# Tile 1's first layer ahead of tile 0's second in a fused attention and MLP kernel, both as seven products of quarters

## The chip, the cores and the metric

The kernel runs on one core of a Trainium2 chip. The metric is the device time of one launch in microseconds (us): 263.96 us, median of three runs (263.92 to 264.14). A core has five engines that work at the same time, each through its own list of instructions in order: TensorE (PE, with PEld for its weight loads), VectorE (DVE), ScalarE (ACT), GpSimd (POOL) and SyncE (SP). They wait for each other through semaphores. Transfers between the chip's memory (DRAM) and the core's SBUF are issued by POOL, SP or ACT and done by 16 DMA engines. Products are summed up in PSUM, which has eight banks of 512 float32 for each of 128 partitions.

## The reference

```python
kv = np.einsum('bhsd,bhse->bhde', k, v)            # 8 batches, 8 heads, 576 rows, 64 wide
out = np.einsum('bhsd,bhde->bhse', q, kv)
rms = np.sqrt(np.mean(out * out, axis=-1, keepdims=True) + 1e-06)
x = (out / rms * g_norm)                           # transposed to 4608 rows of 512
h = x @ w_in                                       # 512 -> 2048
g = h * (1.0 / (1.0 + np.exp(-1.702 * h)))
return (g @ w_out)                                 # 2048 -> 512
```

## The kernel before

**Tiles.** The 4608 rows are worked in nine tiles of 512: tile t has the first 512 rows of batch t, and tile 8 collects the last 64 rows of all eight batches (`x_rem`, the "rest"). Each tile has a first layer (x times w_in, then the gate on ACT, into `gT`) and a second layer (gT times w_out, collected in `osb` and stored). The attention of batch t+1 runs among the products of tile t.

**Plain layers.** Tile 0 has both layers plain, tile 1 the first: 64 products 512 wide each. `Hidden.mm` (L419) issues one of the first layer, `project` (L756) one of the second. w_in's columns are counted in blocks of 128, 0 to 15.

**Layers as seven products of quarters.** All other layers take each matrix as 2 x 2 quarters and form the product from seven products of quarters instead of eight, with sums of quarters made on DVE before and behind (`SevenIn`, L482, for the first layer, in four groups of columns; `Seven`, L558, for the second). Each product of quarters is 4 (first layer) or 16 (second) matmuls 256 wide, 112 in a layer. In a plan, "35" is group 3, product 5. DVE makes the sums of weights once: `ws` of w_in (`w_in_sum`, L439, products 3, 5, 6 and 7), `tw` of w_out (`weight_sum`, L552); sums of x for each tile (`xS`, L462), and sums of gT (`gS`, L580). In a group, ACT or DVE copies a bank out of PSUM (L480), DVE adds banks (L544, L546), ACT gates (L510). In the second layer ACT keeps three results in the tile `qf` (L617); DVE's sums (L625) and one copy (L628) place the four quarters in `osb`. The products 1, 6, 7 and 4 add up in one bank, "x", so each waits until the one before it is kept or placed.

**Order.** The order is written out by hand. `dense` (L725) runs both layers of a tile; the dictionaries u1 and u2 say behind which product a piece of other work is issued (`at1`, `at2`, L940 and L943). All engines take their instructions in the order in which they are issued here, and the tile framework adds the waits: for data, and for a buffer of a pool to come free.

**Attention of batches 0 and 1.** They are loaded by pairs of heads, c = 0 to 3, to `kraw`, `vbuf` and `qraw`. For batch 1 DVE packs q (L96), PE transposes it (L403) and DVE copies it to `qT` (L409); PE makes kv (L221), DVE copies it to `kvb` (L357); PE makes the output (L254), ACT its square (L272), PE adds up by a product with ones ("ss", L329), ACT takes the root (L331), and DVE applies it, which gives x (`apply`, L339 and L343). In tile 0's second layer this stands at steps 9 to 60 of 64.

**Later batches** come through DMA transposes (`transpose_q`, L242): `rows` (L275), `add_up`, `roots`, `turn` (L309), and a DMA transpose of x.

**g_norm** (`g_col`) is applied to x for batch 0 alone. For the rest it is multiplied into w_in, once, behind tile 0's first layer (`scale_w_in`, L188).

**Loads.** POOL issues them: batch 0, w_in in parts, then from L879 w_out and batch 1 in turn, and `load_q` and `load_kv` for batch 2 and on.

**Buffers.** One `gT`, two `osb`, two `qf`, one `gS`; PSUM in pools ps_a (3 banks), ps_h (3) and ps_o (2).

Of the kernel before, what the change touches and what calls it, by code (L numbers as in the profile page):

```python
# [16 lines left out]
def kernel(  # L17
# [27 lines left out]
    GROUP = 6  # L45
# [19 lines left out]
    qbuf = const.tile([P, NPAIR * NJ * P], F16)  # L65
    kraw = const.tile([P, NPAIR, 2 * NJ * D], F16)
# [61 lines left out]
    for n in "kqv":  # L128
        if n != "q":
            rows = stage.tile([P, 6, 2 * P], F32, name="qf", tag="qf", bufs=2)  # L130
# [39 lines left out]
    load_w_in(10, 13)  # L170
    load_w_in(13, FO)
# [16 lines left out]
    def scale_w_in(ko, engine):  # L188
        w = w_in_sb[:, ko]
        if engine is nc.scalar:  # L190
            engine.activation(w, w, AFT.Copy, scale=g_col)
        else:
            engine.tensor_scalar_mul(w, w, g_col)

    class Attention:
# [14 lines left out]
        def kv(self, c):  # L210
            if c % self.KEEP == 0:
                self.kvp = ps_a.tile([P, NPAIR, D], F32, name="kvp", tag="att")
# [123 lines left out]
        def apply(self, c):  # L336
            o, rs, n = self.o[c]
            if c < NPAIR and self.b == 0:
# [12 lines left out]
    class Early(Attention):  # L351
        KEEP = 2
# [12 lines left out]
    class First(Early):  # L365


        ss_pool = (ps_o, "o")
# [23 lines left out]
    class Second(Early):  # L392


        ss_pool = rest_pool = (ps_h, "hT")

# [42 lines left out]
    def w_in_sum(n):  # L439

        a11, a12, a21, a22 = quarters(w_in_sb, slice(0, HF * P), slice(0, KH))
        op, a, b = (
            (nc.vector.tensor_add, a21, a22),
            (nc.vector.tensor_sub, ws[:, 0], a11),
            (nc.vector.tensor_sub, a11, a21),
            (nc.vector.tensor_sub, a12, ws[:, 1]),
        )[n]
        op(ws[:, n], a, b)

    class Sums:  # L450


        def __init__(self, t, x):
            x = x if t < B else x.rearrange("p c (j r) -> p c j r", j=J)
# [103 lines left out]
    class Seven:  # L558
# [3 lines left out]
        LAST = (1, 5, 6, 2, 3, 7, 4)  # L562

        def __init__(self, t, gT):
            self.t, self.gT = t, gT
            self.s = spool.tile([P, 4, HF, 2 * P], F16, name="gS", tag="gS")
            self.bank, self.kept = {}, None

        def sums(self, i0, i1, which=(0, 1, 2, 3)):
# [41 lines left out]
        def keep(self, name, mo, as_):  # L611
            ps, m = self.ready(name, mo)
            if self.kept is None:
                k = stage.tile([P, 6, HN], F32, name="qf", tag="qf", bufs=2)
# [4 lines left out]
        def place(self, name, mo, with_, i, j):  # L619
# [9 lines left out]
            if self.t == B:  # L629
# [3 lines left out]
                elif i == 1:  # L633
                    store_rest(2 + mo, j * HN, (j + 1) * HN)
            elif self.t in HALVED and j == 1 - i:
                store(self.t, 2 * i, 2 * i + 2)

        def run(self, units2):
            n = 0
            self.banks("z", 0)  # L640
            for p in self.LAST if self.t == B else self.ORDER:
# [41 lines left out]
    def hid_seven(t, hid, seven, units1):  # L683
# [8 lines left out]

        gates = []
        for n, step in enumerate(todo.steps):
# [12 lines left out]
            for i0, i1, which in todo.ready.get(n, ()):  # L707
                seven.sums(i0, i1, (which,))
# [7 lines left out]

        left = {n: [lambda x=x: late(x) for x in steps] for n, steps in todo.late.items()}
        end = lambda: seven.sums(HF - 2, HF, (0,))
# [6 lines left out]
    def dense(t, units1, units2, group, deep, hid=None):  # L725
        hid = hid or Hidden(t)
        gT = hid.gT
        seven = None if deep else Seven(t, gT)
        cols = range(FO) if deep else [f for i in range(HF) for f in (i, HF + i)]
        ready = {} if deep else {8: (0, 4), 13: (4, 6), 15: (6, 8, (0,))}  # L730
        if group and t:
            order = [(ko, fo) for part in ((0, 3, 1, 2), range(4, group)) for ko in (0, 1) for fo in part]
            order += [(ko, fo) for ko in range(2, KO) for fo in range(group)]
            for ko, i in order:
                pool = (ps_h, "hT") if i < 3 else (ps_a, "att") if i == 3 else (ps_o, "o")
                hid.mm(ko, cols[i], *pool)
            for i in range(group):
                hid.gate(cols[i])
        left = {}
        if t >= SEVEN:  # L740
            left = hid_seven(t, hid, seven, units1)
            cols = ()
        for i, fo in enumerate(cols):
            if i >= group:
                for ko in range(KO):
                    hid.mm(ko, fo)
                hid.gate(fo)
            for u in units1.get(i, ()):
                u()
            if i in ready:  # L750
                seven.sums(*ready[i])

        osb = osbs[t] = opool.tile([P, 4, DM], F32, name="osb", tag="osb")
        os = {}

        def project(mo, fo):  # L756
            if fo == 0:
                pool, tag = (ps_h, "hT") if mo < 2 else (ps_o, "o")
                os[mo] = pool.tile([P, DM], F32, name="o", tag=tag)
            nc.tensor.matmul(  # L760
                os[mo],
                gT[:, fo, mo * P : (mo + 1) * P],
                w_out_sb[:, fo, :],
                start=(fo == 0),
                stop=(fo == FO - 1),
            )
            if fo == FO - 1:
                copy = nc.scalar.copy if mo % 2 else nc.vector.tensor_copy
                copy(osb[:, mo, :], os[mo])

        if deep:
            steps = [(mo, 4 * i + k) for i in range(3) for mo in range(4) for k in range(4)]
            steps += [(mo, f + k) for f in (12, 14) for mo in range(2) for k in range(2)]
            steps += [(mo, 12 + k) for mo in (2, 3) for k in range(4)]
            for n, (mo, fo) in enumerate(steps):
                project(mo, fo)
                for u in units2.get(n, ()):
                    u()
        else:
            later = plan(t).later if t >= SEVEN else {6: ((6, 8, 1),), 30: ((6, 8, 2), (6, 8, 3))}  # L780
            later = {
                n: [lambda x=x: seven.sums(x[0], x[1], (x[2],)) for x in xs] for n, xs in later.items()
            }
            for n, us in units2.items():
                later.setdefault(n, []).extend(us)
            for n, us in left.items():
                later[n] = us + later.get(n, [])
            seven.run(later)
        if t < EARLY:

            n = 0
            while n < SM:
                mo, j, p = n // P, n // PE_, n % PE_
                m = min((mo + 1) * P, (j + 1) * PE_) - n
                nc.sync.dma_start(
                    out=out[t * S : (t + 1) * S, :][bass.DynSlice(NJ * p + j, m, step=NJ), :],
                    in_=osb[n % P : n % P + m, mo, :],
                )
                n += m
        elif t < B and t not in HALVED:  # L800
            store(t, 0, J)
# [87 lines left out]
    load_w_out(14, FO)  # L889

    osbs = {}
    SEVEN = 2
# [26 lines left out]
    FIRST = {  # L919
        "rows": (1, 7, 14, 20),  # L920
        "add_up": (5, 12, 18, 26),
        "table": 21,
        "roots": (32, 32),
        "turn": (33, 34, 35, 36),
    }

    def plan(t):
        return LATER if t < B - 1 else LAST_TWO
# [7 lines left out]
    for t in range(NT):  # L936
        b = t + 1
        u1, u2 = {}, {}

        def at1(i, f, *args):  # L940
            u1.setdefault(i, []).append(lambda: f(*args))

        def at2(i, f, *args):  # L943
            u2.setdefault(i, []).append(lambda: f(*args))  # L944

        def of(b, name, *args):
            return lambda: getattr(live[b], name)(*args)

        if t == 0:
            at1(7, of(0, "out", NPAIR))  # L950
            at2(4, setattr, a0, "ss_pool", Attention.ss_pool)
            at2(4, of(0, "ss", NPAIR, True))
            at2(4, of(0, "apply", NPAIR))
            at1(8, start, 1)
            at2(5, scale_w_in, 0, nc.scalar)
            at2(6, scale_w_in, 1, nc.scalar)
            at2(33, weight_sum, 0)
            at2(33, scale_w_in, 2, nc.vector)
            at2(34, scale_w_in, 3, nc.vector)
            for n, at in ((2, 35), (0, 39), (1, 40)):  # L960
                at2(at, w_in_sum, n)
            for l in range(2):
                at1(9, nc.vector.memset, kvd[l], 0.0)
            at1(13, load_q, 2)
            for c in range(NPAIR):
# [75 lines left out]
```

## Time and profile before

| | us |
|---|---|
| median of three runs | 263.96 |
| the profiled execution's own time | 263.92 |
| its span, first to last instruction of the program | 262.1 |

| stretch of the span | what PE works on |
|---|---|
| 0 to 16.3 | batch 0's attention, first products |
| 16.3 to 29.0 | tile 0's first layer |
| 29.0 to 47.3 | tile 0's second layer, batch 1's attention among it |
| 47.3 to 62.1 | tile 1's first layer, batch 2's kv |
| 62.1 to 75.5 | tile 1's second layer |
| 75.5 to 208.2 | tiles 2 to 6, 26.6 each |
| 208.2 to 257.4 | tiles 7 and 8 |

Times in the views are microseconds from the span's start, unless marked ns. "L530" is a line of the kernel before. A row of the lines view has line, engine, operation, tiles, shapes and count, then the busy time, the mean ns of one, and the idle time of the engine ahead of them with what ended it. "To landing" is the time from the issue of a DMA until its semaphore tells that the data is there.

### The profile page before, as it was taken

To read this page: it belongs to the slowest core of one execution; us is meant where nothing else is said; L and a number is where in the kernel's file an instruction comes from. 1 tells how busy PE (TensorE), PEld (TensorE's weight loads), DVE (VectorE), ACT (ScalarE), POOL (GpSimd) and SP (SyncE) were. 2 spreads that over 40 slices of the span, in tenths; PEclk is the share of its full clock that TensorE was granted. 3 is DMA by queue.
4 is the path that set the end of the run, shared out by engine and by line. 5 is a ranking of instruction groups with operands and counts; after the bars stand their busy time and mean duration, and the time that the engine had idled before them with its cause. 6 is when DMAs were issued, how large, how long until landed. Compare 5 with 4: busy or idle time off the path is not lost.

```text
span 262.1 us, 6210 instructions
## 1 busy us (share of the span) xinstructions
PE 253.6 (97%) x2556; PEld 204.3 (78%) x2556; DVE 185.1 (71%) x324; ACT 173.6 (66%) x308; POOL 43.7 (17%) x68
## 2 busy tenths in 40 slices
PE   6899999999999999999999999999999999999992
PEld 5434554447888988898889988998899888888882
DVE  1540378868768995899589958995899587567831
ACT  3459836776649963996489748974798469737810
POOL 8863242005005001400050005000000000000000
PEclk9999999999999999999999999999999999999998
DMA  7999999999989946996899769946600620021005
GB/s 173 197 199 205 205 203 177 217 206 130 163 180 172 221 58 160 117 240 83 145 154 196 102 157 150 237 54 154 165 0 8 156 83 0 3 100 63 0 3 160
DMA packets 59806, 35.32 MB, mean 135 GB/s; under 512 B 31554, under 2 KB 57154, under 8 KB 59650
## 3 DMA queue, kind: packets, MB, share of 16 engines
q0 software_dynamic: 28608, 18.17, 50.1%
q1 hardware_dynamic: 30768, 16.36, 27.1%
q8 instruction: 20, 0.33, 0.5%
q10 hardware_dynamic: 402, 0.39, 0.5%
q14 instruction: 8, 0.07, 0.1%
HBM read 36.70 MB, written 9.44 MB: 176 GB/s over the span
## 4 chain that ended last, share of the span: by engine, by line
PE 92%; DMA 4%; POOL 1%; DVE 0%; issue 0%; ACT 0%; ACTq 0%
PE o L648 37%; PE h L530 33%; PE hT L422 10%; PE o L760 5%; PE kvp L221 2%; DMA vbuf<-in_v_dram 2%; DMA qraw<-in_q_dram 2%; PE outR L281 2%; PE ss L329 1%; PE outT L254 0%; PE q L403 0%; PE outT L258 0%; POOL kraw L89 0%; ACT sq L272 0%; DVE osb L628 0%
## 5 line engine op out<-in xcount | busy, mean ns | idle before, releaser
L648 PEld LDWEIGHTS <-gS 128*128 128x128 f16 x512 | 49.8, 98 | 5.5
L510 ACT ACTIVATE gT<-h 128x512 f16<-128x512 f32 x84 | 46.2, 605 | 5.1 <-PE h L530 5.1
L530 PEld LDWEIGHTS <-ws 128*128 128x128 f16 x448 | 43.8, 98 | 5.1
L648 PE MATMUL o<-tw,gS 128*128 128x256 f16 x384 | 46.3, 273 | 0.0
L530 PE MATMUL h<-xS,ws 128*128 128x256 f16 x336 | 45.3, 273 | 0.0
L648 PEld LDWEIGHTS <-gT 128*128 128x128 f16 x384 | 37.1, 98 | 4.2
L530 PEld LDWEIGHTS <-w_in_sb 128*128 128x128 f16 x336 | 32.5, 98 | 3.9
L648 PE MATMUL o<-w_out_sb,gT 128*128 128x256 f16 x256 | 33.3, 273 | 0.0
L422 PE MATMUL hT<-xT,w_in_sb 128*128 128x512 f16 x128 | 28.9, 379 | 0.0
L625 DVE TENSOR_TENSOR osb<-o,qf 128x512 f32<-128x512 f32 (+1 forms) x25 | 16.7, 668 | 15.6 <-PE o L648 12.8
L530 PE MATMUL h<-xT,w_in_sb 128*128 128x256 f16 x192 | 27.1, 273 | 0.0
L89 POOL DMA_DIRECT2D kraw<-in_k_dram x11 | 8.1, 733 | 106.3 <-PE kvp L221 87.8
L580 DVE TENSOR_TENSOR gS<-gT 128x512 f16<-128x512 f16 (+2 forms) x34 | 22.0, 653 | 4.5 <-ACT gT L431 3.9
L544 DVE TENSOR_TENSOR h<-h,s 128x512 f32<-128x512 f32 x28 | 19.5, 698 | 7.4 <-PE h L530 5.6
L422 PEld LDWEIGHTS <-w_in_sb 128*128 128x128 f16 x128 | 12.3, 98 | 15.4 <-issue 0.9
L431 ACT ACTIVATE gT<-hT 128x512 f16<-128x512 f32 x32 | 17.6, 613 | 7.0 <-PE hT L422 7.0
L546 DVE TENSOR_TENSOR s<-h,s 128x512 f32<-128x512 f32 x28 | 19.4, 692 | 4.0 <-PE h L530 3.3
L331 ACT ACTIVATE rs<-ss,eps_t 128x512 f32<-128x512 f32 (+1 forms) x16 | 9.2, 584 | 16.4 <-PE ss L329 16.3
L510 ACT ACTIVATE gT<-s 128x512 f16<-128x512 f32 x28 | 17.3, 628 | 1.2 <-DVE s L546 1.2
L944 ACT ACT_TABLE_LOAD x14 | 18.0, 1283 | 0.3
L681 POOL DMA_DIRECT2D out_dram<-osb x2 | 1.1, 562 | 94.1 <-DVE osb L625 94.1
L760 PE MATMUL o<-w_out_sb,gT 128*128 128x512 f16 x64 | 16.7, 380 | 0.0
(93 smaller groups left out, 367.6 us busy)
## 6 DMA issues: line engine op xcount, KB each, us to landing
out_dram<-osb SPq DMA_DIRECT2D x10, 512.0 KB, 3.5
kraw<-in_k_dram POOLq DMA_DIRECT2D x6, 576.0 KB, 8.7
vbuf<-in_v_dram POOLq DMA_DIRECT2D x6, 576.0 KB, 12.1
qraw<-in_q_dram POOLq DMA_DIRECT2D x3, 512.0 KB, 13.3
qbuf<-in_q_dram POOLq DMA_DIRECT2D x3, 512.0 KB, 14.0
out_dram<-osb SPq DMA_DIRECT2D x6, 192.0 KB, 6.9
w_in_sb<-in_moe_w_in_dram POOLq DMA_DIRECT2D x4, 256.0 KB, 7.5
w_out_sb<-in_moe_w_out_dram POOLq DMA_DIRECT2D x2, 512.0 KB, 14.0
```

The source lines that it names most:

```text
L331: nc.scalar.activation(rs[:, 0:n], t[:, 0:n], AFT.Abs_reciprocal_sqrt, bias=eps_t, scale=1.0 / D)
L422: nc.tensor.matmul(self.h[fo], w_in_sb[:, ko, fo * P : (fo + 1) * P], self.x[:, ko], start=(ko == 0), stop=(ko == KO - 1),)
L431: nc.scalar.activation(self.gT[:, fo, :], self.h[fo], AFT.Gelu_apprx_sigmoid)
L510: nc.scalar.activation(self.gT[:, to, n * TH : (n + 1) * TH], src, AFT.Gelu_apprx_sigmoid)
L530: nc.tensor.matmul(bank[name][:, a], w, x, start=(p in (1, 5) and a == 0 and k == 0), stop=(k == KH - 1), skip_group_check=True,)
L544: nc.vector.tensor_add(bank["z"], bank["x"], self.s5)
L546: nc.vector.tensor_add(self.s5, bank["x"], self.s5)
L580: op(s[:, n, lo], a, b)
L625: nc.vector.tensor_add(o, ps, self.kept[with_][:, m])
L648: nc.tensor.matmul(o, a, w, start=(p in (1, 2, 5) and i == 0 and (mo == 0 or split)), stop=(i == HF - 1), skip_group_check=True,)
L760: nc.tensor.matmul(os[mo], gT[:, fo, mo * P : (mo + 1) * P], w_out_sb[:, fo, :], start=(fo == 0), stop=(fo == FO - 1),)
L944: u2.setdefault(i, []).append(lambda: f(*args))
```

## The change

1. Order: tile 0's first layer, tile 1's first layer, tile 0's second, tile 1's second; from tile 2 on as before (with batch 0's rest worked at tile 7, beside batch 1's).
2. Tile 1's first layer and tile 0's second become seven products of quarters, the first by a new plan, `SECOND`; the second layers of both tiles take the products in a new order, `FIRST = (1, 2, 6, 5, 7, 3, 4)`.
3. Batch 1's attention goes among columns 6 to 15 of tile 0's first layer. The columns 12 and 13 are held: DVE copies them from PSUM to osb[0], and ACT gates them from there later, as it does 14 and 15 (from PSUM) once its gate table is back.
4. Batch 1's loads stand among w_in's, and w_out behind them, in four parts.
5. `w_in_sum` works on column groups g0 to g1, ahead of any scaling. x of batch 1 gets g_col too; w_in and ws are scaled behind tile 1's first layer, six of the eight rows on ACT.
6. Two `gT`, one `osb`, one `qf`; tiles 0 and 1 share one `gS`. Tiles 0 and 1 are stored in halves.

```diff
-    GROUP = 6
+    GROUP, HELD, OPEN = 6, 12, 14
-    gpool = ctx.enter_context(tc.tile_pool(name="gpool", bufs=1))
+    gpool = ctx.enter_context(tc.tile_pool(name="gpool", bufs=2))
-    opool = ctx.enter_context(tc.tile_pool(name="opool", bufs=2))
+    opool = ctx.enter_context(tc.tile_pool(name="opool", bufs=1))
...
-            if c < NPAIR and self.b == 0:
+            if c < NPAIR and self.b < EARLY:
...
-    def w_in_sum(n):
+    def w_in_sum(n, g0, g1):
-        a11, a12, a21, a22 = quarters(w_in_sb, slice(0, HF * P), slice(0, KH))
+        f = slice(2 * g0 * P, 2 * g1 * P)
+        a11, a12, a21, a22 = quarters(w_in_sb, f, slice(0, KH))
...
+        FIRST = (1, 2, 6, 5, 7, 3, 4)
...
+            elif self.t < EARLY and j == 1 - i:
+                store_early(self.t, 2 * i * P, (2 * i + 2) * P)
...
+    def first_columns(hid, units):
+        for i in range(GROUP, FO):
+            for ko in range(KO):
+                hid.mm(ko, i)
+                if ko == 1:
+                    for u in units.get(i - 0.5, ()):
+                        u()
+            if i < HELD:
+                hid.gate(i)
+            elif i < OPEN:
+                nc.vector.tensor_copy(osbs[0][:, i - HELD, :], hid.h[i])
+            for u in units.get(i, ()):
+                u()
...
-    load_w_out(0, 4)
-    early_load("q", 1, 0, NPAIR)
-    load_w_out(4, 8)
+    early_load("q", 1, 0, 2)
+    load_w_in(10, 12)
     early_load("k", 1, 0, 2)
-    load_w_out(8, 10)
-    load_w_out(10, 12)
     early_load("v", 1, 0, 2)
-    early_load("k", 1, 2, NPAIR)
-    early_load("v", 1, 2, NPAIR)
-    load_w_out(12, 14)
-    load_w_out(14, FO)
+    load_w_in(12, 15)
+    early_load("q", 1, 2, 4)
+    for c in (2, 3):
+        early_load("k", 1, c, c + 1)
+        early_load("v", 1, c, c + 1)
+    load_w_in(15, FO)
+    for f in range(0, FO, 4):
+        load_w_out(f, f + 4)
...
+    SECOND = Plan(
+        "01 11 05 02 06 15 21 03 12 07 16 35 25 22"
+        " 26 04 31 17 27 36 14 23 13 33 37 32 24 34",
...
+    at(6, a0.keep_rest)
+    at(7, start, 1)
+    for c in (0, 1):
+        at(7, of(1, "pack_q", c))
+        at(9 + c, of(1, "q", c))
+        at(11, of(1, "kv", c))
+        at(12, of(1, "out", c))
+        at(13, of(1, "pack_q", 2 + c))
+    for n in range(4):
+        at(8 if n < 2 else 10, w_in_sum, n, 0, 2)
+        at(12, w_in_sum, n, 2, 3)
+    at(11, table, ROOT)
+    for c in (0, 1):
+        at(13, of(1, "ss", c))
+    for c in (0, 1):
+        at(13, of(1, "q", 2 + c))
+    at(13, of(1, "apply", 0))
+    at(13, of(1, "kv", 2))
+    at(13, of(1, "apply", 1))
+    at(14, of(1, "kv", 3))
+    at(14, of(1, "out", 2))
+    at(14.5, of(1, "out", 3))
+    at(15, of(1, "ss", 2))
+    at(15, of(1, "apply", 2))
+    first_columns(d0, u)
...
+    at(0, of(1, "ss", 3))
+    at(0, of(1, "apply", 3))
+    at(0, table, GELU)
+    for i in range(OPEN, FO):
+        at(0, d0.gate, i)
+    begin(at, 1, 2)
+    for i, n in enumerate((4, 8)):
+        at(n, gate_held, d0, HELD + i)
+    for n in range(4):
+        at(6, w_in_sum, n, 3, 4)
+    at(22, sevens[0].sums, 0, 4, 0, 1)
+    at(24, weight_sum, 0)
+    left = first_layer(1, u, sevens[0].s)
...
+    at(0, weight_sum, 1)
+    for n, ko in ((16, 0), (48, 1), (64, 2), (82, 3)):
+        at(n, scale, w_in_sb[:, ko], nc.scalar)
+    at(33, weight_sum, 2)
+    at(35, weight_sum, 3)
+    at(72, of(2, "kv_all", "D"))
+    ask(at, 78, 3)
+    at(82, sevens[1].sums, 0, 8, 0)
+    at(86, sevens[1].sums, 0, 8, 1)
+    for n in range(2):
+        at(98, scale_sum, n, nc.vector)
+    second_layer(0, u, {}, {1: ((4, 8, 0, 1),), 34: ((0, 8, 2, 3),)})
+    u, at = hooks()
+    attend(at, 2, LATER.attn)
+    for n in range(2, 4):
+        at(16 * n + 16, scale_sum, n, nc.scalar)
+    begin(at, 100, 3)
+    second_layer(1, u, left, {20: ((0, 8, 2),), 58: ((0, 8, 3),)})
```

`ask` loads a batch (`load_kv`, `load_q`), `begin` starts it with its DMA transposes of q, `attend` sets rows, sums, roots and turns at the steps of the plan as before, `table` loads ACT's table. `second_layer` is `Seven.run` with these hooks.

More of the change, by code (lines that the diff above doesn't have):

```diff
@@ L65 @@
     qbuf = const.tile([P, NPAIR * NJ * P], F16)
+    q_rest = const.tile([P, NPAIR, R], F16)
     kraw = const.tile([P, NPAIR, 2 * NJ * D], F16)
@@ L129 @@
         if n != "q":
-            rows = stage.tile([P, 6, 2 * P], F32, name="qf", tag="qf", bufs=2)
+            pool, tag, n1 = (opool, "osb", 8) if n == "v" else (stage, "qf", 6)
+            rows = pool.tile([P, n1, 2 * P], F32, name=tag, tag=tag, bufs=1)
             rows = rows.rearrange("p h x -> p (h x)")[0:PE_]
@@ L211, in kv @@
             if c % self.KEEP == 0:
-                self.kvp = ps_a.tile([P, NPAIR, D], F32, name="kvp", tag="att")
+                pool, tag = (ps_o, "o") if self.b < EARLY and c > 1 else (ps_a, "att")
+                self.kvp = pool.tile([P, NPAIR, D], F32, name="kvp", tag=tag)
             self.kv_product(self.kvp[:, c, :], c)
@@ L691, in product @@
             return parts[int(step[0])].product(int(step[1]))
+        for i in range(4):
+            if todo.xsums[i] < 0:
+                xs.form(i)
         gates = []
@@ L723, in hid_seven @@
         return left
[L725 to L748, printed above, removed]
-                u()
[L750 to L765, printed above, removed]
-            )
[L767 to L801, printed above, removed]
@@ new lines, with first_layer, second_layer @@
+    sevens = {}
+    def first_layer(t, units, s=None):
+        hid = Hidden(t)
+        sevens[t] = Seven(t, hid.gT, s)
+        return hid_seven(t, hid, sevens[t], units)
+    def second_layer(t, units, left, later):
+        if t:
+            osbs[t] = opool.tile([P, 4, DM], F32, name="osb", tag="osb")
+        seven = sevens[t]
+        todo = {n: [lambda x=x: seven.sums(*x) for x in xs] for n, xs in later.items()}
+        for n, us in units.items():
+            todo.setdefault(n, []).extend(us)
+        for n, us in left.items():
+            todo[n] = us + todo.get(n, [])
+        seven.run(todo)
+        if EARLY <= t < B and t not in HALVED:
+            store(t, 0, J)
@@ L917 @@
     )
[L919 to L925, printed above, removed]
     def plan(t):
-        return LATER if t < B - 1 else LAST_TWO
+        return SECOND if t < EARLY else LATER if t < B - 1 else LAST_TWO
     HALVED = (2, 3, 4, 5, 6)
@@ new lines, in hooks, with of, table, attend @@
+    def hooks():
+        units = {}
+        return units, lambda n, f, *args: units.setdefault(n, []).append(lambda: f(*args))
+    def of(b, name, *args):
+        return lambda: getattr(live[b], name)(*args)
+    def table(name):
+        nc.scalar.preload_act_table_set(name)
+    ROOT, GELU = "abs_reciprocal_sqrt_and_small", "gelu_apprx_sigmoid_and_others"
+    def attend(at2, b, at):
+        at2(at["table"], table, ROOT)
+        for h in range(2):
+            at2(at["roots"][h], of(b, "roots", h))
+        for j in range(J):
+            for name in ("rows", "add_up", "turn"):
+                at2(at[name][j], of(b, name, j))
+        at2(46, of(b, "out", NPAIR))
+        at2(74, of(b, "ss", NPAIR))
+        at2(80, of(b, "apply", NPAIR))
+        at2(82, table, GELU)
@@ new lines, in ask, with begin @@
+    def ask(at, n, b):
+        at(n, load_kv, b)
+        at(n, load_q, b)
+    def begin(at, n, b):
+        at(n, start, b)
+        at(n, of(b, "transpose_q"))
+    osbs[0] = opool.tile([P, 4, DM], F32, name="osb", tag="osb")
+    sevens[0] = Seven(0, d0.gT)
+    u, at = hooks()
+    at(6, a0.keep_rest)
+    for l in range(2):
+        at(6, nc.vector.memset, kvd[l], 0.0)
+    at(7, start, 1)
[5 more added lines that the diff above has]
+        at(13, of(1, "pack_q", 2 + c))
@@ new lines @@
+    for n in range(2, 4):
+        at(16 * n + 16, scale_sum, n, nc.scalar)
+    begin(at, 100, 3)
+    second_layer(1, u, left, {20: ((0, 8, 2),), 58: ((0, 8, 3),)})
+    for t in range(EARLY, NT):
+        b = t + 1
+        todo = plan(t)
+        u, at = hooks()
+        if b < B:
+            at(todo.steps.index("kv"), of(b, "kv_all", todo.keep))
+        if t + 2 < B:
+            ask(at, 15, t + 2)
+        left = first_layer(t, u)
+        u, at = hooks()
+        if b < B:
+            attend(at, b, todo.attn)
+        elif t < B:
+            for r, n in ((0, 16), (1, 36)):
+                at(n, setattr, live[r], "ss_pool", (ps_a, "att"))
+                at(n, of(r, "out", NPAIR))
+                at(n + 14, of(r, "ss", NPAIR))
+                at(n + 18, of(r, "apply", NPAIR))
+            at(26, table, ROOT)
+            at(56, table, GELU)
+        if t + 2 < B:
+            begin(at, 100, t + 2)
+        second_layer(t, u, left, todo.later)
```

138 lines of the change are left out of this document (49 added, 89 removed).

## The prediction

> **What bounds the kernel now.** I read the page's busy shares and chain of waits first, then the chain in order of time, then the windows of the first 50 us.
>
> ```profile
> PE 253.6 (97%) x2556; PEld 204.3 (78%) x2556; DVE 185.1 (71%) x324; ACT 173.6 (66%) x308; POOL 43.7 (17%) x68
> PE 92%; DMA 4%; POOL 1%; DVE 0%; issue 0%; ACT 0%; ACTq 0%
> ```
>
> TensorE (PE) is the bound: 92% of the chain that ends last. A change can gain only by taking PE work away, and it loses wherever PE is made to wait. The chain's pieces (start, us, what) price that work and date the stages:
>
> ```profile
> 22.06 6.91 PE hT L422 x32
> 31.24 0.26 PE q L403 x6
> 38.10 0.31 PE kvp L221 x12
> 47.31 10.36 PE hT L422 x48
> 57.67 0.88 PE kvp L221 x48
> 62.33 0.22 PE outR L281 x4
> 75.46 0.87 PE h L530 x8
> 89.34 1.31 PE o L648 x12
> ```
>
> A plain product (512 wide) takes 10.36/48 = 0.216 us, a quarter product (256 wide) 1.31/12 = 0.109. Tile 2 starts at 75.46; from there the schedule stays as it is. So I ask when the changed kernel reaches that point.
>
> ```profile
> 0.00:10.00 10.00, 7.28 (x126) 5.21 (x126) 2.97 (x11) 2.71 (x3) 8.39 (x20) 1.00 0.96 182
> 10.00:22.00 12.00, 10.93 (x92) 5.04 (x92) 5.21 (x11) 8.43 (x14) 8.28 (x12) 1.00 1.34 199
> 22.00:29.00 7.00, 7.00 (x36) 3.13 (x32) 0.00 (x0) 5.44 (x11) 2.03 (x3) 1.00 1.28 205
> 29.00:47.30 18.30, 18.30 (x146) 9.08 (x145) 13.39 (x24) 11.43 (x14) 5.49 (x7) 1.00 1.30 193
> ```
>
> Per window: length, busy PE, PEld, DVE, ACT, POOL, granted clock, DMA share, GB/s. PE is full from 22 on and the loads run at 200 GB/s throughout. VectorE (DVE) does nothing from 22 to 29: batch 1's attention sits at 29 to 47.3, under tile 0's 64 plain second-layer products, which can run whether or not batch 1 has come.
>
> **What the change removes.** Two layers go from 64 x 0.216 = 13.8 us to 112 x 0.109 = 12.2: 1.6 saved each, 3.2 in all. The stretch 28.97 to 47.31 is 18.3 us long and holds 13.8 of products and 4 x (0.26 + 0.31 + 0.216 + 0.216) = 4.0 of attention, so at most 0.5 of waits can go too. Batch 0's remainder moves to tile 7 and adds about 0.3 there (four 64-wide products, one sum, their bank waits). The most it can give is 3.4.
>
> **Stage one: batch 1's attention now stands ahead of everything else.** Its 4.0 us of PE work comes among columns 8 to 15 of tile 0, and tile 1's first layer cannot start without it. First the loads, in POOL's new order:
>
> ```profile
> L153 POOL DMA_DIRECT2D w_in_sb<-in_moe_w_in_dram x1: 742/742/742, 11.7 to 11.7; - x1
> ...
> DMA to landing us min/median/max: 8.3/8.3/8.3
> ```
> ```profile
> kraw<-in_k_dram POOLq DMA_DIRECT2D x6, 576.0 KB, 8.7
> ```
>
> w_in's columns 8-9 land at 11.7 + 8.3 = 20.0. Up to there the queue is unchanged; behind it I add sizes at 200 KB/us (half a batch's q, k or v is 288 KB, a column block of w_in, 512 x 128 in two bytes, 128): q half 21.5, columns 10-11 22.8, k and v halves 25.7, columns 12-14 27.6, second q half 29.0, k and v of pairs 2 and 3 30.5 and 31.9, column 15 32.6, w_out 42.8, batch 2 51.5. In the built order each load waits for the eighth before it, which lands at least 5 us ahead of its own turn, so the queue does not run dry.
>
> PE starts column 8 at 21.8, does columns 8-11, two q's and two kv's by 26.4, and then stands until 27.6 for column 12, which ends at 28.5. From there DVE is the chain. Its durations:
>
> ```profile
> L480 DVE COPY s<-h 128x512 f32<-128x512 f32 x11 | 7.5, 683 | 2.7 <-PE h L530 2.7
> L544 DVE TENSOR_TENSOR h<-h,s 128x512 f32<-128x512 f32 x28 | 19.5, 698 | 7.4 <-PE h L530 5.6
> L580 DVE TENSOR_TENSOR gS<-gT 128x512 f16<-128x512 f16 x18 | 7.4, 418 | 0.9 <-ACT gT L431 0.9
> L462 DVE TENSOR_TENSOR xS<-xT 128x512 f16<-128x512 f16 x12 | 5.0, 421 | 1.2 <-DMA xT<-x 1.1
> L448 DVE TENSOR_TENSOR ws<-w_in_sb 128x2048 f16<-128x2048 f16 x2 | 2.4, 1220 | 0.0
> L339 DVE SCALAR_TENSOR_TENSOR xT<-outT,g_col,rs 128x512 f16<-128x512 f32 x4 | 3.0, 744 | 1.7 <-ACT rs L331 1.7
> L309 DVE TENSOR_TENSOR x<-outR,sum 128x512 f16<-128x512 f32 x24 | 14.9, 683 | 0.8 <-ACT sum L305 0.8
> L409 DVE COPY qT<-q 128x576 f16<-128x576 f16 x4 | 1.8, 455 | 1.1 <-PE q L403 1.1
> L357 DVE CAST kvb<-kvp 64x128 f16<-64x128 f32 x4 | 1.2, 288 | 1.3 <-PE kvp L221 1.3
> L331 ACT ACTIVATE rs<-ss,eps_t 128x512 f32<-128x512 f32 x8 | 5.4, 694 | 2.9 <-PE ss L329 2.9
> L191 ACT ACTIVATE w_in_sb<-w_in_sb,g_col 128x2048 f16<-128x2048 f16 x2 | 3.9, 1990 | 0.0
> L272 ACT ACTIVATE sq<-outT 128x512 f16<-128x512 f32 x8 | 4.7, 595 | 10.0 <-PE outT L254 9.9
> ```
> ```profile
> 29.50 1.39 DVE L96 COPY qbuf<-qraw 96x768 f16<-96x768 f16 x4 [10.49 <-DMA qraw<-in_q_dram]
> ```
>
> Back to back, DVE instructions overlap by some 0.05 (four packs of 0.406 take 1.39). In DVE's built order: copy of the held column 12 (0.65) to 29.3; four weights' sums of 512 elements (0.37 each; not in the trace with rows of 256, taken as L580's 128x512, with the 1220 ns for four times the elements, 0.31, below it) 30.8; held column 13 31.5; two packs 32.2; the last two qT copies with PE's transposes between them 33.5; two applies (0.7 each) with four short kvb copies among them (0.25 each, taken near the upper bound: L357 has twice the elements, the lower end is half of it, 0.14) 35.9. Then the output of pair 3 on PE and its square on ACT 36.9, the root of pair 2 37.6, the third apply 38.4, xS 38.8, a bank copy 39.4, the fourth apply 40.1. Only then can the fourth product of tile 1 ("02") go on. PE has then issued 12 quarter products; without a wait they would be out at 21.8 + 32 x 0.216 + 4.0 + 12 x 0.109 = 34.0. **Loss 6.1 us.** The same work waited nowhere before, because the second layer covered it.
>
> The other 100 products take 10.9, to 51.0; DVE has eight sums of banks and three copies at 0.65, three xS, four weights' sums and two gS, 11.0 in all, and the last product waits for its last: 51.6. ScalarE (ACT) falls some 3 us behind here with four extra gates and a table load, but nothing in the next layer needs it before its first product ends. Tile 0's second layer, 12.2 plus batch 2's kv 0.88, ends at **64.7**. DVE just keeps up with it (p4 needs the p7 sum at 62.9 and gets it at 62.9). The scalings moved behind (four w_in rows and two ws on ACT at L191's 1.99, 12 us of it over two layers of 26) lie between ACT's bank copies; they cost up to 2 if one came ahead of a copy in need, and I take nothing.
>
> **Stage two: one osb buffer.** The pool goes from two to one, and gpool takes the room. In the built program DVE's first write of tile 1's osb (the sum behind product 2) waits for all eight stores of tile 0, and behind it on DVE stand the four turns of batch 2 and the gS that product 3 needs; product 7 is broken by an ss whose bank that same sum frees. In tiles 2 on, a whole first layer lies between. So the landing of the stores matters:
>
> ```profile
> L795 SPq DMA_DIRECT2D out_dram<-osb x1: 346/346/346, 45.3 to 45.3; - x1
> ...
> DMA to landing us min/median/max: 8.0/8.0/8.0
> ```
> ```profile
> L795 SPq DMA_DIRECT2D out_dram<-osb x1: 490/490/490, 49.3 to 49.3; - x1
> ...
> DMA to landing us min/median/max: 7.0/7.0/7.0
> ```
> ```profile
> L795 SPq DMA_DIRECT2D out_dram<-osb x1: 524/524/524, 76.9 to 76.9; - x1
> ...
> DMA to landing us min/median/max: 2.4/2.4/2.4
> ```
> ```profile
> L122 POOL DMA_DIRECT2D qrem<-in_q_dram x1: 990/990/990, 36.3 to 36.3; - x1
> ...
> DMA to landing us min/median/max: 9.9/9.9/9.9
> ```
> ```profile
> L89 POOL DMA_DIRECT2D kraw<-in_k_dram x1: 772/772/772, 58.9 to 58.9; - x1
> ...
> DMA to landing us min/median/max: 6.2/6.2/6.2
> ```
>
> The same eight stores took 8.0 us each beside a load and 2.4 alone. Beside: at 36.3 + 9.9 = 46.2 the queue had 1152 KB of batch 2's k and v left, the stores began at 45.3, and the last landed at 49.3 + 7.0 = 56.3, 10.1 after 46.2. In the changed kernel batch 3's load is asked at step 78, goes out when kv_all has read kraw (60.4), and its k lands 6.2 later, at 66.6, with v and q, again 1152 KB, behind it; the stores start when DVE has done two gS of 1.15 and product 3's sum, at 66.0. So the last lands near 66.6 + 10.1 = 76.7. The sum is done at 77.4, four turns (L309, 0.66 each overlapped) 80.0, gS 81.2, and products 3 and 4 (32 x 0.109) end at **84.6**. Without the wait: 64.7 + 0.6 for the bank that ACT's last copy frees + 112 x 0.109 + 4 x 0.22 for the rows + 0.3 for batch 2's remainder and ss = 78.7. With it PE stands from 74.6 (product 7 broken behind step 74) to 77.4 and again, ss and five products later, from 78.1 to 81.2. **Loss 5.9.**
>
> **Sum.** 84.6 - 75.46 = 9.2 later, 0.3 at tile 7: 9.5. The profiled run took 263.92 (span 262.1 and 1.8 around it), within 0.04 of the median: **273.4**. Errors: landing of the stores (the 2.4 row would put it at 72.3, product 3 is then held 1.5 and the time is 268.9; full durations instead of overlapped ones add about 2). Own range 268.5 to 276.
>
> [...]
>
> **Rivals.**
> - *Faster:* both waits are hidden. For it: DVE is idle from 22 to 29 and half its chain could go there. Against: columns 12 on land at 27.6, behind that gap. It decides if stage one loses under 2 and the stores land by 72. 263.92 - 3.4 = 260.5. Chance 0.12.
> - *Stores land in time:* only stage one is lost. For: 2.4 us when alone. Against: the load goes out 6 us earlier. 78.7 - 75.46 + 0.3 = 3.5: 267.4. Chance 0.10.
> - *Stage one is hidden, the stores are not:* 273.4 - 6.1 = 267.3. Chance 0.04.
> - *The clock falls* in the pauses and 32 products take double: up to 3.5 more, 276.9. Chance 0.08, as the pauses come near 3 us and no trace shows the fall.
> - *The products do not save* (quarters held by weight loads): excluded here, 0.109 holds in every later tile.
>
> **How the numbers follow.** My forecast has 0.65; 0.01 is left for no change. Less than 0.2% is what this kernel's measurement cannot tell. Faster 0.12, same 0.01, slower 0.87. The range 266.5 to 276 leaves out the faster case and half of the clock's.
>
> **What would show it.** Tile 2's first product near 84.6, with the span's start to tile 1's fourth product near 40; DVE full from 28 to 36 while PE has gaps; POOL's w_in columns 12-14 landing near 27.6; a DVE wait at the first osb sum of tile 1 on a DMA of osb near 76.7; PE idle before ss and before product 3. A DVE chain that reaches the fourth apply by 36, or stores landed by 72, would make me wrong.

## The result, and the profile after

The changed kernel takes 276.36 us (median of four runs, 275.53 to 277.25), the kernel before 264.05 beside it (four runs, 263.92 to 265.88): a ratio of 1.045, 95% interval 1.039 to 1.051. The profiled execution has a span of 274.4 against 262.1, so 12.3 more. The forecast was 273.4; the time lies 0.4 above the upper end of its range.

Three rows of the page first: busy time by engine, the granted clock in 40 slices, and the shares of the chain that ends last.

```profile
PE 255.6 (93%) x2652; PEld 215.1 (78%) x2652; DVE 201.4 (73%) x357; ACT 183.9 (67%) x318; POOL 44.5 (16%) x70
PEclk9999999999986999999999999999999999999999
PE 75%; DMA 9%; DVE 9%; POOL 3%; issue 2%; SPq 2%; ACT 0%; DVEq 0%
```

PE's share of the chain falls from 92% to 75%, and DMA and DVE have 18% where they had 4. New in the middle of the kernel is also the clock: two slices below full speed, one ending and one beginning at about 82 us. PE's timeline shows the waits that matter below, each at the row that it delays (start, duration, idle before it and what released it):

```profile
28.35 1.04 PE L423 MATMUL hT<-xT,w_in_sb 128*128 128x512 f16 x4 [1.02 <-DMA w_in_sb<-in_moe_w_in_dram]
...
32.50 0.43 PE L404 MATMUL q<-ident,qbuf 96*128 96x96 f16 x6 [1.29 <-DVE qbuf L97]
...
40.81 0.49 PE L532 MATMUL h<-xT,w_in_sb 128*128 128x256 f16 x3 [0.38 <-DVE xT L340]
...
66.40 0.38 PE L654 MATMUL o<-w_out_sb,gT 128*128 128x256 f16 x2 [0.67 <-ACT osb L631]
...
78.28 0.27 PE L330 MATMUL ss<-sq,ones 128*128 128x256 f16 x1 [2.53 <-DVE osb L628]
...
81.81 3.60 PE L654 MATMUL o<-w_out_sb,gS 128*128 128x256 f16 x16 [2.71 <-DVE gS L583]
85.19 2.78 PE L654 MATMUL o<-tw,gT 128*128 128x256 f16 x16
```

Tile 1's fourth product goes on at 40.8, behind the fourth apply (DVE xT L340). The two late pauses stand where they were forecast, ahead of the ss and ahead of product 3. But the last two rows are new: the first 16 products take 3.38 us up to the next row, 0.211 each, where the later tiles have 0.109 (12 in 1.31 at 101.86). DVE's timeline names what stands behind the two pauses:

```profile
77.54 0.69 DVE L628 TENSOR_TENSOR osb<-o,qf 128x512 f32<-128x512 f32 x1 [5.95 <-DMA out_dram<-osb]
78.15 2.47 DVE L310 TENSOR_TENSOR x<-outR,sum 128x512 f16<-128x512 f32 x4
80.54 1.21 DVE L583 TENSOR_TENSOR gS<-gT,gS 128x2048 f16<-128x2048 f16 x1
```

DVE stands 5.95 us for tile 0's stores, then does four turns and the gS that product 3 needs. The stores' issues (count and time of issue) and their landing:

```profile
L779 SPq DMA_DIRECT2D out_dram<-osb x8: 345/510/1279, 66.8 to 71.3; - x8
...
DMA to landing us min/median/max: 5.9/6.5/7.0
```

The chain of waits ends this stretch so; tile 2 starts at 87.98, where the kernel before had 75.46:

```profile
71.34 5.88 DMA out_dram<-osb
...
81.81 6.17 PE o L654 x32
87.98 0.87 PE h L532 x8
```

And the windows (length, busy PE, PEld, DVE, ACT, POOL, granted clock, DMA share, GB/s) show why 32 products took 6.17:

```profile
72.50:81.80 9.30, 4.07 (x39) 3.26 (x37) 4.26 (x7) 6.89 (x7) 0.00 (x0) 0.91 0.73 147
81.80:86.00 4.20, 4.19 (x20) 3.02 (x21) 1.44 (x3) 0.00 (x0) 0.00 (x0) 0.50 0.40 76
86.00:88.00 2.00, 2.00 (x16) 1.60 (x14) 0.46 (x2) 0.00 (x0) 0.00 (x0) 0.76 0.44 127
```

The granted clock is at 0.50 from 80.1, within the second pause, until 87.0: 6.17 in place of 32 x 0.109 = 3.5, 2.7 lost.

### The profile page after: what moved, and what is told of

The parts are those of the page before. It is cut to its first block, busy times and chain, and to the rows that moved or that the text cites. A ratio compares the mean times of both kernels' runs of the same rounds, so it can differ in the third digit from the quotient of the medians.

```text
span 274.4 us, 6457 instructions
## 1 busy us (share of the span) xinstructions
PE 255.6 (93%) x2652; PEld 215.1 (78%) x2652; DVE 201.4 (73%) x357; ACT 183.9 (67%) x318; POOL 44.5 (16%) x70
## 4 chain that ended last, share of the span: by engine, by line
PE 75%; DMA 9%; DVE 9%; POOL 3%; issue 2%; SPq 2%; ACT 0%; DVEq 0%
PE o L654 36%; PE h L532 33%; DMA w_in_sb<-in_moe_w_in_dram 7%; DMA out_dram<-osb 2%; PE kvp L222 2%; PE outR L282 2%; SPq L779 2%; DVE gS L583 1%; DVE ws L450 1%; DVE xT L340 1%; POOL qraw L90 1%; DVE x L310 1%; DVE osb L628 1%; POOL kraw L90 1%; POOL vbuf L90 1%
## 5 line engine op out<-in xcount | busy, mean ns | idle before, releaser
L654 PEld LDWEIGHTS <-gS 128*128 128x128 f16 x576 | 56.6, 99 | 12.7 <-DVE gS L583 3.0
L512 ACT ACTIVATE gT<-h 128x512 f16<-128x512 f32 x96 | 52.8, 604 | 5.1 <-PE h L532 5.1
L532 PEld LDWEIGHTS <-ws 128*128 128x128 f16 x512 | 50.1, 98 | 6.9 <-issue 1.0
L532 PE MATMUL h<-xS,ws 128*128 128x256 f16 x384 | 51.7, 273 | 0.4 <-DVE xS L464 0.3
L654 PE MATMUL o<-tw,gS 128*128 128x256 f16 x432 | 51.7, 273 | 0.0
L532 PEld LDWEIGHTS <-w_in_sb 128*128 128x128 f16 x384 | 37.1, 98 | 6.1 <-issue 1.3
L654 PE MATMUL o<-w_out_sb,gS 128*128 128x256 f16 x144 | 18.9, 289 | 2.7 <-DVE gS L583 2.7
L532 PE MATMUL h<-xS,w_in_sb 128*128 128x256 f16 x128 | 18.8, 273 | 0.0
L620 ACT COPY qf<-o 128x512 f32<-128x512 f32 (+1 forms) x29 | 16.0, 553 | 3.6 <-PE o L654 3.1
L654 PE MATMUL o<-tw,gT 128*128 128x256 f16 x144 | 18.1, 281 | 0.0
```

The source lines that it names most:

```text
L512: nc.scalar.activation(self.gT[:, to, n * TH : (n + 1) * TH], src, AFT.Gelu_apprx_sigmoid)
L532: nc.tensor.matmul(bank[name][:, a], w, x, start=(p in (1, 5) and a == 0 and k == 0), stop=(k == KH - 1), skip_group_check=True,)
L620: nc.scalar.copy(self.kept[as_][:, m], ps)
L654: nc.tensor.matmul(o, a, w, start=(p in (1, 2, 5) and i == 0 and (mo == 0 or split)), stop=(i == HF - 1), skip_group_check=True,)
```

## The experiments

Each was run once beside the kernel before (263.7 to 264.2 us), the ninth four times. Spans are compared with spans: 274.4 for the changed kernel. Its four runs span 273.8 to 275.4, so where two versions differ by less than some 1.6, the conclusion rests on the rows shown and not on the span.

**e1: tile 0's results in buffers of their own.** The four `s5` buffers of the pool `stage`, idle in tile 0's second layer, take its results.

```diff
+            if self.t == 0:
+                for a in range(m.start, m.stop):
+                    o, p = out0[2 * i + a][:, j * HN : (j + 1) * HN], ps[:, a - m.start]
...
-                in_=osbs[t][n % P : n % P + m, mo, :],
+                in_=out0[mo][n % P : n % P + m] if t == 0 else osbs[t][n % P : n % P + m, mo, :],
```

> Tile 0's results go to the four s5 buffers of the stage pool (2 KB each, free from about 52.5 to 88) instead of the single osb buffer; DVE and ACT place them in halves of 256, so each placement costs some 0.15 us more. Nothing else changes. Theory (the wait for tile 0's eight stores): DVE's first osb sum of tile 1 no longer waits for a DMA, PE has no pause around ss, its clock stays at 1.00, and tile 2 starts near 79.5 to 80 instead of 87.98; span 274.4 - 8.2 = 266.2. Rival (DVE is late there anyway, the stores only end last by chance): the pause stays in good part and the span falls by less than 3.

Measured: 275.1 us, span 272.7. PE's timeline of this version:

```profile
81.48 1.04 PE L532 MATMUL h<-xT,w_in_sb 128*128 128x256 f16 x8
...
97.49 1.03 PE L282 MATMUL outR<-kvd,qTd 128*128 128x128 f16 x8 [2.49 <-DMA qTd<-qbuf]
```

Both late pauses are gone, the clock is 1.00 there, and tile 2 starts at 81.48, 6.3 earlier (87.81 in the same view of the changed kernel). The span gained 1.7. What took most of the rest stands in the second row: a pause for batch 3's q, transposed by a DMA that now goes out in the same moment as batch 4's load:

```profile
L245 SPq DMA_TRANSPOSE qTd<-qbuf x1: 3174/3174/3174, 83.8 to 83.8; - x1
...
DMA to landing us min/median/max: 13.7/13.7/13.7
```

During that pause the clock falls to 0.50 a second time, for 3.41 us, which costs more (columns as in the windows above):

```profile
97.01:100.42 3.41, 2.93 (x20) 2.47 (x21) 1.63 (x3) 1.68 (x3) 0.00 (x0) 0.50 1.31 263
```

So the wait for the stores was real, and undoing it made a transfer late that the delay had kept apart from the load. Besides, stage one was 1.6 later (fourth product at 42.4): w_in's columns landed 0.7 later, and the clock was at 0.50 from 28.7 to 32.2.

**e2: batch 3's load only after the stores** (a read of `kraw` on ACT at step 47 holds it).

```diff
-    ask(at, 78, 3)
...
+    late = const.tile([P, 1], F16, name="late")
+    at(47, nc.scalar.copy, late[0:PE_, :], kraw[0:PE_, 0, 0:1])
+    ask(at, 47, 3)
```

> Batch 3's load is held back: ACT reads one column of kraw behind step 47 of tile 1's second layer (about 73.5), and the load of k, which overwrites kraw, can only go out after that, instead of at 61.6. Theory (the stores land late because they share the DMA engines with that load): the eight stores land 2.0 to 3 us after their issue instead of 5.9 to 7.0, the last at 73.5 to 74.5 instead of 77.2, and tile 2 starts 3 to 5.5 us earlier; span 269 to 271.4. Rival (eight stores of 64 to 192 KB take that long by themselves): they land as before, span 274.4 or, if batch 3's k then comes late to tile 2, longer.

Measured: 280.78 us, span 279.0: slower, where a gain was expected; 1.6 of it is stage one, late as in e1. The stores did what was expected of them:

```profile
DMA to landing us min/median/max: 1.9/2.6/3.2
```

Without a load beside them they land in 2.6 us (median) and not in 6.5. But the load, out at 75.7, now lay beside batch 2's two DMA transposes of x (12.5 us, median of both) that tile 2 starts from:

```profile
89.22 1.89 PE L532 MATMUL h<-xT,w_in_sb 128*128 128x256 f16 x8 [5.76 <-DMA xT<-x]
```

**e3: the two late pauses filled with idle products** of 256 columns, whose results nobody reads.

```diff
...
+    at(73, warm, 20)
+    at(79, warm, 22)
```

> 42 idle products 256 wide (20 ahead of ss, 22 ahead of product 3) into an unused half of a PSUM bank fill PE's two pauses in tile 1's second layer; no wait is taken away. Theory (the pauses halve the granted clock, which then holds for products 3 and 4): the clock stays at 1.00, the 32 products take 3.5 us instead of 6.17, tile 2 starts near 85.3 and the span is 271.7, though PE does more. Rival (the 32 products are slow from something else, the DMA transposes or their weight loads): they still take about 6.2 and the span stays at 274.4 or grows.

Measured: 273.56 us, span 271.8. PE does more and the span is 2.6 shorter. The chain of waits:

```profile
81.39 3.67 PE o L655 x32
85.06 0.87 PE h L533 x8
```

3.67 where there were 6.17, with the clock at 1.00 from 80 to 88. The clock rival is thereby shown, with its price.

**e4: the held columns' two copies on ACT** instead of DVE.

```diff
-                nc.vector.tensor_copy(osbs[0][:, i - HELD, :], hid.h[i])
+                nc.scalar.copy(osbs[0][:, i - HELD, :], hid.h[i])
```

> The copies of the held columns 12 and 13 from PSUM go to ACT, which has little to do there, instead of DVE. Theory (from column 12 on DVE's chain sets stage one): DVE's packs come about 1.3 us earlier, the fourth product of tile 1 goes on near 39.5 instead of 40.8, the stage behind it moves by as much, span 273.1. Rival (the loads set it: the last k, v and column 15 land at 32.6 and 33.4): the fourth product moves by less than 0.3 and the span stays.

Measured: 277.1 us, span 274.6. The packs did start earlier, at 29.79 and not at 32.10, but not what follows them. PE's timeline:

```profile
30.11 1.91 PE L423 MATMUL hT<-xT,w_in_sb 128*128 128x512 f16 x4
31.82 0.97 PE L330 MATMUL ss<-sq,ones 128*128 128x512 f16 x2
32.63 0.42 PE L404 MATMUL q<-ident,qbuf 96*128 96x96 f16 x6
```

Column 13 takes 1.91 in place of 1.03: here too the clock was at 0.50 from 29.2 to 32.6, and the time saved on DVE was spent on PE. The transposes start at 32.63 (changed kernel: 32.50). That left the theory open, and e6 repeats it with the clock held.

**e5: e1 with batch 3's q transposes ahead of tile 1's first stores** in SP's queue.

```diff
-    begin(at, 100, 3)
+    begin(at, 84, 3)
```

> Tile 0's results in buffers of their own, as in the first experiment (span 272.7), and batch 3's two q transposes asked at step 84 of tile 1's second layer in place of step 100, so ahead of tile 1's first stores in SP's queue. In the first experiment tile 2 began at 81.5 and not at 88.0, but the transposes went out at 83.8, beside batch 4's load (83.7), took 13.7 us, and tile 2's second layer waited for them until 97.5. Theory: that wait is all that hid the gain of the buffers; the transposes now go out at 79.9, when q has landed, and take 4 to 5 us; tile 2 takes its usual 26.6 us from 81.5 on: tile 3 at 108.1 in place of 112.6, span 268.1, or 266.5 if the clock doesn't fall between 28 and 33. Rival: tile 2 is limited by batch 4's load as a whole (stores and transposes crowd each other wherever they stand): span 271 or more.

Measured: 270.41 us, span 268.4. The q transposes went out at 79.4, and the pause at 97.5 is gone. Here the clock was at 0.50 from 14.4 to 17.8 and from 34.8 to 38.2 (0.985 over the run), and the fourth product came at 42.05. That one line of order is worth 4.3 (0.3 of it from stage one), so the theory holds.

**e6: e3 with e4's copies on ACT and eight idle products** in the pauses ahead of batch 1's first kv and of column 12.

```diff
...
+            if self.b == 1 and c == 0:
+                warm_on(self.kvp.rearrange("p c d -> p (c d)"), 4)
...
+                if fo == HELD:
+                    warm_on(self.h[fo], 4)
...
```

> The version with idle products in the two late pauses (span 271.8), with the two held columns' copies on ACT, and eight idle products ahead of batch 1's first kv (4 of 256) and of column 12 (4 of 512). Alone, the copies on ACT moved the packs from 32.1 to 29.8 but the clock fell to 0.50 between 28.5 and 33 and PE reached the transposes behind them at 32.6 instead of 32.5. Theory: the clock took that gain; with the clock held, the transposes start at 31.2, the fourth product of tile 1 goes on at 39.5 instead of 40.8, span 270.5. Rival: the chain behind the packs waits for v of pairs 2 and 3 (landed 31.2 and 32.7) and nothing moves: 271.8.

Measured: 272.5 us, span 270.7, 1.1 less than e3. PE's timeline:

```profile
31.22 0.42 PE L419 MATMUL q<-ident,qbuf 96*128 96x96 f16 x6
...
39.51 0.49 PE L549 MATMUL h<-xT,w_in_sb 128*128 128x256 f16 x3 [0.38 <-DVE xT L355]
```

Transposes at 31.2 and the fourth product at 39.5, as the theory had it: DVE's order ahead of the packs was on the path, for 1.3.

**e7: e3 without batch 1's pairs 2 and 3** (left out, tile 1's first layer reads quarters 0 and 1 in their place).

```diff
-        at(13, of(1, "pack_q", 2 + c))
...
-    at(13, of(1, "kv", 2))
...
+            self.x = [[x[:, k : k + KH, n : n + 2, :] for n in (0, 2)] for k in ((0, 0) if t == 1 else (0, KH))]
...
```

> Left out: batch 1's pairs 2 and 3 (packs, transposes, kv, outputs, roots, applies), tile 1's first layer reads quarters 0 and 1 in their place; idle products in the late pauses as in the third experiment (span 271.8). It prices the wait of stage one. Theory: nothing else holds the start of tile 1's first layer; its fourth product goes on at 34 to 35 (column 15 lands at 33.4) instead of 40.8, and all behind it moves by 6 to 6.8: tile 2 at 78.5, span 265.2 to 266. Rival: the next limit is near (the DVE sums of the first layer, w_out's landing at 43.6, batch 2's k and v at 53.2): less than 4 us of it arrive at tile 2, span over 268.

Measured: 269.37 us, span 267.5, between the two: 4.3 less than e3. PE's timeline first, with column 15 and the fourth product, then the chain of waits at tile 2:

```profile
33.46 1.04 PE L424 MATMUL hT<-xT,w_in_sb 128*128 128x512 f16 x4 [1.41 <-DVE xT L341]
...
35.72 0.60 PE L533 MATMUL h<-xT,w_in_sb 128*128 128x256 f16 x4
```
```profile
77.00 3.67 PE o L655 x32
80.67 0.87 PE h L533 x8
```

The fourth product goes on at 35.7, 5.1 earlier, and 4.4 of that arrive at tile 2 (80.67 against e3's 85.06). So of the way from 34.0 (the forecast's no-wait point) to 40.8, pairs 2 and 3 cost 5.1, PE's own work for them included; 1.7 stay without them. There column 15 stands 1.41 us until 33.46, where its weights land (33.4) and the second apply ends too; which of the two holds it isn't settled.

**e8: e6 with the second half of batch 1's q loaded, packed and transposed ahead of column 12.**

```diff
-    load_w_in(12, 15)
     early_load("q", 1, 2, 4)
+    load_w_in(12, 15)
...
```

> The stage-one version with the clock held (copies on ACT, idle products) and, besides, the second half of batch 1's q loaded ahead of w_in's columns 12 to 14, its packs and transposes ahead of column 12 on DVE and PE. Theory: the second q is what starts the late chain; packed at 27 to 28, the limit is v of pair 3 (landed 32.7), and with PE's work from column 12 on (5.8 us from 29.7) the fourth product goes on at 37.5: 2 us less than the version beside it, 3.3 less than the changed kernel: span 268.5. Rival: columns 12 to 14 land 1.4 later, hold DVE's sums of w_in and PE's columns, and the gain is eaten: 270.5 or more.

Measured: 272.75 us, span 271.0: the rival's number, but not by its cause. Columns 12 to 14 landed 1.0 later and PE went on with them; what held was a bank:

```profile
33.48 0.38 PE L236 MATMUL kvp<-vbuf,kraw 96*64 96x64 f16 x12 [0.69 <-ACT rs L347]
...
39.98 0.49 PE L549 MATMUL h<-xT,w_in_sb 128*128 128x256 f16 x3 [0.38 <-DVE xT L355]
```

The kv of pair 2 needs one of two ps_o banks, both held by the ss until ACT has taken its roots; and ACT, with the two copies moved to it, came to the first only at 32.7.

**e9: e5 and e6's stage one together.**

> The own buffers and the turned q transposes (span 268.4, fourth product of tile 1 at 42.05) together with the stage-one version whose clock is held (copies on ACT, eight idle products; fourth product at 39.5). Theory: the two losses stand one behind the other and add up; all moves 2.5 earlier: span 265.9, some 267.9 by the times, still 1.4% above the kernel before, since tile 1's first layer still waits for batch 1's pairs 2 and 3 (worth 4.3 where they were left out). Rival: with stage one earlier a load (batch 2's k and v at 53.2, batch 3's) is next and less than 1.2 arrives: span over 267.2.

Measured: 267.19 us (267.06 to 267.55) against 264.09, ratio 1.012, 95% interval 1.010 to 1.014; span 265.3, clock 1.00. PE's timeline has one wait left between the fourth product and tile 2:

```profile
65.16 0.38 PE L680 MATMUL o<-w_out_sb,gT 128*128 128x256 f16 x2 [0.79 <-ACT s L648]
...
78.50 1.04 PE L548 MATMUL h<-xT,w_in_sb 128*128 128x256 f16 x8
```

The effects add up, 0.6 better than expected. Of the 12.3 lost, 9.1 are back without giving up the new order. The rest is stage one: without any wait the forecast's count puts tile 2 at 84.6 - 6.1 - 5.9 = 72.6; here it starts at 78.5, 5.9 later, and 5.4 of that is the fourth product at 39.4 in place of 34.0, a point that the loads alone rule out (below). No version tried here beats the kernel before.

**e10 and e11: only one of the two late pauses filled.** e10 keeps the 20 idle products of the first, e11 the 22 of the second.

> Idle products in the first of the two late pauses alone (20 of 256 wide ahead of the ss; with both filled the span was 271.8 and the 32 products behind took 3.67; with none 274.4 and 6.17). Theory: a pause counts by its own length: the second, 2.7 us, is no longer than others that left the clock at 1.00, so the clock holds with either one filled: 271.8. Rival: the second pause alone takes the clock down: 274.4, products 6.2.

Measured: 276.36 us, span 274.6: no gain at all, so the theory fell. PE's timeline:

```profile
81.46 3.60 PE L655 MATMUL o<-w_out_sb,gS 128*128 128x256 f16 x16 [2.71 <-DVE gS L584]
```

The clock was at 0.50 from 80.3 to 87.1. That other pauses of 2.7 us left it at 1.00, as the expectation has it, is not shown: the late pause that by itself did so, in e11, is 2.23 us long.

> Idle products in the second of the two late pauses alone (22 of 256 wide behind product 7). Theory: the first pause, 2.5 us, does not take the clock down by itself: 271.8, the 32 products 3.7. Rival: the fall begins in the first pause, and the idle products run at 0.50 themselves, so that most of the slow stretch lies under the pause anyway: clock under 1.00 from 78 to 82, span 271.8 to 272.8.

Measured: 273.6 us, span 271.8, and the clock is at 1.00 from 74 to 88 (0.998 over the run):

```profile
81.63 1.92 PE L655 MATMUL o<-w_out_sb,gS 128*128 128x256 f16 x16 [0.31 <-DVE gS L584]
```

In one run each, the clock fell to 0.50 with the second pause alone, 2.71 us (e10), and stayed at 1.00 with the first alone, 2.23 (e11).

## Why the prediction was right and where it missed

*Direction and places: right.* Both losses were where they were put: e1, e2 and e5 show the one by taking the wait for the stores away, e6 and e7 the other by making the chain ahead of tile 1 shorter. (Three slips in the working: 84.6 - 75.46 is 9.1 and not 9.2; the four packs overlap by 0.08 each, by their own figures, and not by 0.05; and the eight stores beside a load took 6.9 to 8.0 us, not 8.0 each.)

*The saving:* a quarter product took 0.109 with the clock at 1.00, as used (12 in 1.31 at 101.86 in the changed kernel).

*Stage one: right in kind, 0.7 short.* Columns 12 to 14 landed at 28.3 (forecast 27.6) and the chain on DVE kept that lag: fourth product 40.8 for 40.1. The step "From there DVE is the chain" held: two copies off DVE moved it by 1.3 (e6). The no-wait point of 34.0 was too kind: the weights of column 15 land at 33.4 (the prediction's own list has 32.6), and with its four products and tile 1's first twelve (0.9 + 1.3) 35.6 is the earliest; e7 has 35.7. That changed nothing in the sum, which needs only the 40.1.

*Stage two: right, and in part by luck.* The last store landed at 77.2 (forecast 76.7), the sum was done at 78.2 (77.4), product 3 began at 81.8 (81.2). The cause is shown too: 2.6 us alone in e2 and 6.5 beside the load. The term was taken from another load of the same size, but its two parts missed in opposite directions: the load went out at 61.6 and its k landed at 68.1, 1.5 later than forecast, and the last store came 9.1 behind that and not 10.1.

*The clock: the step that failed.* The forecast gave it 0.08, "as the pauses come near 3 us and no trace shows the fall", and left it out of the sum. No row that the forecast read shows the doubling that the rival's 3.5 rests on; the run shows 0.50 and 6.17 for the 32 products. The fall came, and cost 2.7 of the 12.3; e3 gives 2.6 of them back. So the time came out nearer to that rival's 276.9 than to the forecast of 273.4. With the clock the parts close: 9.1 + 0.6 (product 3 later) + 2.7 = 12.4, where tile 2 is 12.5 late (87.98 - 75.46); behind it come 0.2 less, where 0.3 more was expected, and why is open. That no trace shows the fall was a misreading: the kernel before has one in its tail, where nothing waits for it, at 259.98. PE had been busy for 24% of the 3.41 us ahead, as in the changed kernel (76.73 to 80.14, below), and idle for 2.6 us:

```profile
256.57:259.98 3.41, 0.81 (x8) 0.47 (x5) 0.82 (x2) 0.00 (x0) 0.00 (x0) 1.00 0.88 254
259.98:262.05 2.07, 0.00 (x0) 0.00 (x0) 0.00 (x0) 0.00 (x0) 0.00 (x0) 0.50 0.07 19
```

*The faster rival* asked for both waits to be hidden. The gain of 3.4 that it named was not reached even by e9, where the stores cost nothing: stage one still holds.

## What to carry to other kernels

A pause of TensorE can cost more than its length: here the clock was at 0.50 for 6.8 us behind a fall within a pause of 2.7 (e10, 80.3 to 87.1). Do not go by the longest gap alone (in e4 no pause ahead of the fall at 29.2 was over 1.1 us, and in e11 one of 2.23 left the clock at 1.00), look in the trace for the granted clock, and fill a pause with idle products where nothing useful can stand. When a wait is taken away, check which transfers go out earlier and what they now run beside: beside a batch load, the stores took 2.5 times as long here (6.5 us in the changed kernel against 2.6 in e2) and the transposes of x four times (12.5 in e2 against 3.2, the median in the changed kernel). Work that was covered by a layer which needs nothing from it becomes the path as soon as its consumer is put in that layer's place.

## What the runs showed of the hardware that was not expected

The clock fell to 0.50 behind stretches in which PE was busy for up to 59% of the time. The windows date the falls: 80.1 in the changed kernel, 80.3 in e10, 28.7 in e1, 29.2 in e4, and 14.4, the first of two, in e5. A whole stretch at 0.50 lasted 3.41 us in e1 (97.01 to 100.42, the row at e1); PE's busy time (first number behind the length) in the 3.41 us ahead of each fall, in this order:

```profile
76.73:80.14 3.41, 0.82 (x6) 0.48 (x5) 2.60 (x5) 2.73 (x3) 0.00 (x0) 1.00 0.07 5
```
```profile
76.85:80.26 3.41, 1.48 (x13) 0.93 (x10) 3.07 (x6) 2.42 (x3) 0.00 (x0) 1.00 0.01 0
```
```profile
25.35:28.76 3.41, 1.65 (x33) 0.90 (x30) 2.55 (x7) 2.47 (x3) 1.27 (x2) 1.00 1.31 200
```
```profile
25.75:29.16 3.41, 1.67 (x30) 0.97 (x29) 2.80 (x9) 1.88 (x2) 1.33 (x2) 1.00 1.31 201
```
```profile
10.95:14.36 3.41, 2.00 (x29) 1.10 (x30) 2.36 (x5) 1.35 (x3) 1.83 (x3) 1.00 1.21 179
```

That is 24%, 43%, 48%, 49% and 59% busy. In e1 and e4 no single pause before the fall was longer than 1.14 us. The clock came back 3.4 us later there (32.2 and 32.6) and 6.8 later in the late pauses (87.0 in the changed kernel, 87.1 in e10). Why 3.4 in the one place and 6.8 in the other, no run here shows.

PE's busy share alone does not decide, though. A stretch as long over e11's first pause was 42% busy, less than four of the five above, and the clock stayed at 1.00, as it did in the stretch behind it:

```profile
76.12:79.53 3.41, 1.43 (x14) 1.27 (x14) 2.17 (x4) 3.03 (x4) 0.00 (x0) 1.00 0.30 27
79.53:82.94 3.41, 3.10 (x29) 2.55 (x27) 2.98 (x5) 0.66 (x1) 0.00 (x0) 1.00 0.75 138
```

Nearly the same pauses as in e4 at 26 to 34 us left the clock at 1.00 in the changed kernel's own profile, where this stretch was 46% busy, less than e1's 48% and e4's 49%:

```profile
30.08:33.49 3.41, 1.58 (x12) 0.67 (x11) 3.06 (x9) 1.97 (x4) 2.12 (x3) 1.00 1.39 198
```

What else the clock goes by is open.
